# Backward pass of a gated long-convolution block: tile transposes on TensorE, or as DMA transposes

## The chip, the cores and the metric

One Trainium2 chip, one of its cores. The time is the device time of one execution of the whole program, in microseconds (us), as the median of several executions.

A core has these engines: PE (TensorE, matrix multiply, with its own weight loads PEld), DVE (VectorE), ACT (ScalarE), POOL (GpSimd) and SP (SyncE, which here only issues transfers). Sixteen DMA engines per core move data between the chip's main memory (DRAM tensors) and the on-chip SBUF. "PEclk" is the share of TensorE's full clock that the throttle granted. "DMA share" is the mean busy share of the sixteen DMA engines.

## The reference, cut to what matters

The reference computes a block and all its gradients: `jax.vjp` of

```python
xn = layernorm(q)                            # 2048 x 1024
kv = shift_conv(k, shift_k) * v              # 4 taps
y  = irfft(rfft(kv) * rfft(ssm_k)) + kv * ssm_D      # long convolution over 2048
s  = xn * y
g  = silu(((xn @ w_gate) * (xn @ w_up)) @ w_down)    # 1024 -> 3584 -> 1024
out = q + s * g
```

with ten outputs: `out` and nine gradients. Everything is bf16. The Fourier transforms are done as matmuls with cosine and sine tables, so nearly all the arithmetic is TensorE work. In this kernel each matmul takes both operands with the summed axis on the 128 partitions, hence many operands are needed in both orientations; that is where transposes come from.

## The kernel before

Transfers go alternately to two queues, that of SP (hardware issue) and that of POOL (software issue). Each queue is in order.

```python
dma_engs = [nc.sync, nc.gpsimd]
def dma(out, in_, eng=None):        # cut: picks dma_engs in turn
    return eng.dma_start(out=out, in_=in_)
```

All transposes go through one helper: TensorE transposes up to eight 128x128 blocks into PSUM, and ScalarE or VectorE copies each block to SBUF.

```python
def transpose_blocks(pspool, srcs, dst_fn, nblk, tagname):
    for g0 in range(0, nblk, 8):
        nt = min(8, nblk - g0)
        pst = pspool.tile([P, 8 * P], BF16, name=tagname)
        for i in range(nt):
            nc.tensor.transpose(pst[:, i * P:(i + 1) * P], srcs[g0 + i], ident[:])
        for i in range(nt):
            nc.any.tensor_copy(dst_fn(g0 + i), pst[:, i * P:(i + 1) * P])
```

The stages in order of time: layer norm, shift convolution and tables; KV transform (with XNT, the transposed normalised input, built after it); gate and up matmuls; inverse transform; down matmul (`ps_bm`); DY transform (with DBMT, the transposed gradient, built after it); seven groups of the feed-forward backward pass; an inverse transform; the gradient of `w_down` (HH, the transposed hidden tensor) together with the `dk` work; the gradient of the input (`ps_dxn`) in two halves; a last inverse transform.

The first half of a group is called the dh phase here, the second half the dw phase:

```python
for fg in range(FG):                                     # 7 groups
    WDT = fgb.tile([P, DC, 512], BF16, name="WDT")       # one buffer
    for fi in range(4):
        wrow = fgl.tile([P, D], BF16, name="wrow")
        dma(wrow[:], B_w_down[...])
        transpose_blocks(ftps, [... wrow ...], ... WDT ..., DC, "pst_fg")
    DG = ...; DU = ...                                   # [P, NB, 512], one buffer each
    for fi in range(4):                                  # dh phase
        dma(gt_t[:], GTd[frs, :]); dma(ut_t[:], UTd[frs, :])
        for sq in range(SQ):
            # 8 matmuls ps_dh <- WDT, DBMT; ScalarE copies ps_dh to dh_b
            nc.vector.tensor_tensor(dgt[:, cs], dh_b[:], ut_t[:, cs], ALU.mult)
            nc.vector.tensor_tensor(dut[:, cs], dh_b[:], gt_t[:, cs], ALU.mult)
        dma(DGTd[frs, :], dgt[:]); dma(DUTd[frs, :], dut[:])
        for (src, dst) in ((dgt, DG), (dut, DU)):
            transpose_blocks(ftps, [... src ...], ... dst ..., NB, "pst_fg")
        p1_tick(fg * 4 + fi)                             # a slice of the spectral products
    for (src, o_w) in ((DG, o_dwg), (DU, o_dwu)):        # dw phase
        # 128 matmuls ps_dw <- src, XNR each; out to o_w
```

Of the kernel before, what the change touches and what calls it, by code (L numbers as in the profile page):

```python
# [12 lines left out]
BF16 = mybir.dt.bfloat16  # L13
# [4 lines left out]
def build_kernel(  # L18
# [6 lines left out]
    nc = tc.nc  # L25
    P = 128
    _, S, D = A_q.shape
    F = B_w_gate.shape[1]
# [3 lines left out]
    NB = S // P  # L32
    DC = D // P
    FC = F // P
    DH = D // 512
    FG = F // 512
    SQ = S // 512
# [26 lines left out]
    def dma(out, in_, eng=None):  # L64
        if eng is None:
            eng = dma_engs[_dma_ctr[0] % len(dma_engs)]
            _dma_ctr[0] += 1
        return eng.dma_start(out=out, in_=in_)  # L68
# [367 lines left out]
# [8 lines that stand above are left out]
# [139 lines left out]
    XNT = xtp.tile([P, DC, S], BF16, name="XNT")  # L583

    def build_xnt():
        with tc.tile_pool(name="xt_ld", bufs=2) as xtl, \
                tc.tile_pool(name="xt_ps", bufs=2, space=bass.MemoryType.PSUM) as xps:
            for sb in range(NB):
                xn_t = xtl.tile([P, D], BF16, name="xn_l2")
                dma(xn_t[:], XNd[sb * P:(sb + 1) * P, :])  # L590
                transpose_blocks(xps, [xn_t[:, dc * P:(dc + 1) * P] for dc in range(DC)],
                                 lambda i, sb=sb: XNT[:, i, sb * P:(sb + 1) * P], DC, "pst_x")

    with tc.tile_pool(name="kvpool", bufs=1) as kvpool, \
            tc.tile_pool(name="twpool_f", bufs=2) as twpool, \
# [221 lines left out]
    def build_dbmt():  # L817
        for sb in range(NB):
            dma(XNR[:, sb, :], XNd[sb * P:(sb + 1) * P, :])
        with tc.tile_pool(name="db_sb", bufs=3) as dbs, \  # L820
                tc.tile_pool(name="db_ps", bufs=2, space=bass.MemoryType.PSUM) as dps:
            for sb in range(NB):
                rs = slice(sb * P, (sb + 1) * P)
                dbm = dbs.tile([P, D], BF16, name="dbm_l")
                dma(dbm[:], DBMd[rs, :])
                transpose_blocks(dps, [dbm[:, dc * P:(dc + 1) * P] for dc in range(DC)],
                                 lambda i, sb=sb: DBMT[:, i, sb * P:(sb + 1) * P], DC, "pst_db")

    with tc.tile_pool(name="dypool", bufs=1) as dypool, \
            tc.tile_pool(name="twpool_b", bufs=2) as twpool, \  # L830
# [57 lines left out]
    if True:  # L888
        with tc.tile_pool(name="fg_big", bufs=1) as fgb, \
# [7 lines left out]
            for fg in range(FG):  # L897
                f0 = fg * 512
                WDT = fgb.tile([P, DC, 512], BF16, name="WDT")
                for fi in range(4):  # L900
                    wrow = fgl.tile([P, D], BF16, name="wrow")
                    dma(wrow[:], B_w_down[f0 + fi * P:f0 + (fi + 1) * P, :])
                    transpose_blocks(ftps, [wrow[:, ddc * P:(ddc + 1) * P] for ddc in range(DC)],
                                     lambda i, fi=fi, WDT=WDT: WDT[:, i, fi * P:(fi + 1) * P], DC, "pst_fg")
                DG = fgb.tile([P, NB, 512], BF16, name="DG")
                DU = fgb.tile([P, NB, 512], BF16, name="DU")
                for fi in range(4):
# [18 lines left out]
                    dma(DGTd[frs, :], dgt[:])  # L926
                    dma(DUTd[frs, :], dut[:])
                    for (src, dst) in ((dgt, DG), (dut, DU)):
                        transpose_blocks(ftps, [src[:, sb * P:(sb + 1) * P] for sb in range(NB)],
                                         lambda i, dst=dst, fi=fi: dst[:, i, fi * P:(fi + 1) * P], NB, "pst_fg")  # L930
                    p1_tick(fg * 4 + fi)
                for (src, o_w) in ((DG, o_dwg), (DU, o_dwu)):
                    for dc in range(DC):
# [93 lines left out]
    wbcp = tc.alloc_tile_pool(name="wbc_pool", bufs=1)  # L1027
    WBC["t"] = build_wbc(wbcp, "Wbc2")
    with tc.tile_pool(name="dwd_big", bufs=1) as dwb, \
            tc.tile_pool(name="dwd_ld", bufs=2) as dwl, \  # L1030
            tc.tile_pool(name="dwd_out", bufs=2) as dwo, \
            tc.tile_pool(name="dk_sb", bufs=2) as dkp, \
# [8 lines left out]
        for fg in range(FG):  # L1041
            for _ in range(per_fg):
                if dk_blocks:
                    dk_block(dk_blocks.pop(0), dkp, psSH)
            HH = dwb.tile([P, NB, 512], BF16, name="HH")
            for fi in range(4):
                fc = fg * 4 + fi
                ht_t = dwl.tile([P, S], BF16, name="ht_t2")
                dma(ht_t[:], HTd[fc * P:(fc + 1) * P, :])
                transpose_blocks(wtps, [ht_t[:, sb * P:(sb + 1) * P] for sb in range(NB)],  # L1050
                                 lambda i, HH=HH, fi=fi: HH[:, i, fi * P:(fi + 1) * P], NB, "pst_hh")
            for fi2 in range(0, 4, 2):
                pss = [wps.tile([P, D], F32, name=f"ps_dwd{k}") for k in range(2)]
                for sb in range(NB):
# [16 lines left out]
    with tc.tile_pool(name="wt_pool", bufs=1) as wtp, \  # L1071
# [11 lines left out]
        for dh in range(DH):  # L1083
# [1 line left out]
            WGT = wtp.tile([P, FC, 512], BF16, name="WGT")  # L1085
            WUT = wtp.tile([P, FC, 512], BF16, name="WUT")
            for (wsrc, wdst) in ((B_w_gate, WGT), (B_w_up, WUT)):
                for di in range(4):
                    dc = dh * 4 + di
                    wnat = wtl.tile([P, F], BF16, name="wnat")  # L1090
                    dma(wnat[:], wsrc[dc * P:(dc + 1) * P, :])
                    transpose_blocks(wtps, [wnat[:, fc * P:(fc + 1) * P] for fc in range(FC)],
                                     lambda i, wdst=wdst, di=di: wdst[:, i, di * P:(di + 1) * P], FC, "pst_wt")
            for sb in range(NB):
                rs = slice(sb * P, (sb + 1) * P)
                dgt_l = dgl.tile([P, FC, P], BF16, name="dgt_l")
# [137 lines left out]
```

## Time and profile before

3121.07 us, median of 2 runs (3117.57 to 3124.57).

| | before |
|---|---|
| TensorE busy | 88% of the span, granted clock 0.935 |
| ScalarE busy | 1060 us |
| feed-forward groups | 1281.3 to 2018.1 us, 737 us |
| a steady group | 95.7 us, for 384 matmuls of 0.216 us = 82.9 us |

Two parts of the page of the kernel before: busy time by engine, and its DMA queues (packets, MB, share of the sixteen engines' time). q1 is the hardware-issued queue of SP, q0 the software-issued queue of POOL:

```profile
PE 2728.1 (88%) x13818; PEld 1281.9 (41%) x13818; DVE 1626.6 (52%) x3829; ACT 1060.1 (34%) x2938; POOL 626.8 (20%) x1049
q1 hardware_dynamic: 304406, 312.36, 30.9%
q0 software_dynamic: 88400, 312.02, 27.9%
```

The load is even between the two queues, about 312 MB each. The columns of the windows view are: busy time and count by engine, granted clock, DMA share, GB/s.

```profile
core 0: us, PE busy (x) PEld busy (x) DVE busy (x) ACT busy (x) POOL busy (x), PEclk, DMA share, GB/s
1731.80:1768.90 37.10, 36.02 (x244) 18.52 (x244) 21.93 (x77) 27.18 (x95) 4.82 (x9) 1.00 0.63 203
1769.80:1826.60 56.80, 56.62 (x278) 26.25 (x278) 2.80 (x12) 14.03 (x36) 4.86 (x9) 1.00 0.20 72
```

The reader is to see that the group's mean share of 0.36 is made of 0.63 and 0.20.

### The profile page before, as it was taken

The numbers are of one execution on the slowest core, as the hardware profiler recorded it, in microseconds if no ns is written. First come the engines' busy times: TensorE is split into PE (matmuls) and PEld (weight loads), VectorE is DVE, ScalarE is ACT, GpSimd is POOL, SyncE is SP. The second block draws the span as 40 slices with busy tenths as digits, with TensorE's granted clock in tenths as the row PEclk, the third lists the DMA queues.
The fourth block names the chain that finished last, engine by engine and source line by source line (L and its number), as shares of the span: only waits on it lengthen the run. The fifth ranks groups of instructions, "written<-read, shape, count | busy, mean of one in ns | idle before, by whom it ended". The sixth has DMA issues, their size and how long they took to land. (4 is left out here: it accounts for less than half of the span.)

```text
span 3117.5 us, 39882 instructions
## 1 busy us (share of the span) xinstructions
PE 2728.1 (88%) x13818; PEld 1281.9 (41%) x13818; DVE 1626.6 (52%) x3829; ACT 1060.1 (34%) x2938; POOL 626.8 (20%) x1049
## 2 busy tenths in 40 slices
PE   4949899999799979799899999878899599889888
PEld 2413344444344434444444444433444344444333
DVE  7977778111255751299953331184997460034461
ACT  6512433333101113545535543300555530242222
POOL 2221132222334320112110110133221111112200
PEclk8978999999899989899999999998999689889988
DMA  7795595343748882588644432266875685558602
GB/s 250 286 334 193 193 322 216 145 167 117 280 156 288 284 295 102 185 299 280 214 168 140 141 127 92 94 224 208 296 264 178 213 250 158 161 162 244 210 25 84
DMA packets 393008, 626.92 MB, mean 201 GB/s; under 512 B 147795, under 2 KB 260435, under 8 KB 388964
## 3 DMA queue, kind: packets, MB, share of 16 engines
q1 hardware_dynamic: 304406, 312.36, 30.9%
q0 software_dynamic: 88400, 312.02, 27.9%
q8 instruction: 108, 1.77, 0.2%
q14 instruction: 94, 0.77, 0.1%
HBM read 406.89 MB, written 221.55 MB: 202 GB/s over the span
## 5 line engine op out<-in xcount | busy, mean ns | idle before, releaser
L429 PE MATMUL psI<-YSh,TWR 128*128 128x512 bf16 x1536 | 355.9, 391 | 69.5 <-DVE TWR L217 19.1
L688 PE MATMUL psG<-XNT,wg_s 128*128 128x512 bf16 x896 | 342.7, 383 | 11.3 <-ACT g_b L691 6.8
L689 PE MATMUL psU<-XNT,wu_s 128*128 128x512 bf16 x896 | 342.6, 382 | 3.2 <-DMA wu_s<-in_B_w_up_dram 3.0
L1105 PE MATMUL ps_dxn<-WGT,dgt_l 128*128 128x512 bf16 x896 | 341.6, 382 | 0.0
L1105 PE MATMUL ps_dxn<-WUT,dut_l 128*128 128x512 bf16 x896 | 340.9, 381 | 0.2 <-DMA dut_l<-DUTd 0.2
L936 PEld LDWEIGHTS <-XNR 128*128 128x128 bf16 x1792 | 174.9, 98 | 212.7 <-issue 9.1
L429 PEld LDWEIGHTS <-TWR 128*128 128x128 bf16 x1536 | 152.2, 100 | 262.0 <-issue 64.5
L920 PE MATMUL ps_dh<-DBMT,WDT 128*128 128x512 bf16 x896 | 221.3, 390 | 9.8 <-ACT WDT L443 8.7
L1058 PE MATMUL ps_dwd<-DBM,HH 128*128 128x512 bf16 x896 | 206.2, 382 | 12.1 <-ACT HH L443 7.4
L936 PE MATMUL ps_dw<-DG,XNR 128*128 128x512 bf16 x896 | 199.9, 381 | 3.9 <-ACT w_b L939 3.0
L756 PE MATMUL ps_bm<-WD,ht_t 128*128 128x512 bf16 x896 | 195.7, 381 | 3.7 <-DMA ht_t<-HTd 3.7
L936 PE MATMUL ps_dw<-DU,XNR 128*128 128x512 bf16 x896 | 194.9, 379 | 1.6 <-ACT w_b L939 1.5
L695 DVE TENSOR_TENSOR h_b<-g_b,u_b 128x512 bf16<-128x512 bf16 x112 | 47.4, 423 | 225.6 <-ACT u_b L693 225.6
L939 ACT CAST w_b<-ps_dw 128x512 bf16<-128x512 f32 x112 | 65.3, 584 | 267.3 <-PE ps_dw L936 257.7
L691 ACT CAST g_b<-psG 128x512 bf16<-128x512 f32 x112 | 65.5, 585 | 256.4 <-PE psG L688 239.7
L689 PEld LDWEIGHTS <-wu_s 128*128 128x128 bf16 x896 | 88.3, 99 | 117.7 <-issue 10.8
L688 PEld LDWEIGHTS <-wg_s 128*128 128x128 bf16 x896 | 88.2, 98 | 112.3 <-issue 8.7
L443 ACT COPY HH<-pst_hh 128x128 bf16<-128x128 bf16 x441 | 117.2, 266 | 50.0 <-PE pst_hh L441 38.0
L756 PEld LDWEIGHTS <-ht_t 128*128 128x128 bf16 x896 | 87.7, 98 | 111.7 <-issue 4.6
L1105 PEld LDWEIGHTS <-dut_l 128*128 128x128 bf16 x896 | 88.0, 98 | 106.6 <-issue 1.6
L1105 PEld LDWEIGHTS <-dgt_l 128*128 128x128 bf16 x896 | 88.1, 98 | 105.2 <-issue 1.1
L1058 PEld LDWEIGHTS <-HH 128*128 128x128 bf16 x896 | 84.7, 98 | 110.8 <-ACT HH L443 15.2
(341 smaller groups left out, 4574.9 us busy)
## 6 DMA issues: line engine op xcount, KB each, us to landing
kt<-KPAD SPq DMA_DIRECT2D x64, 256.0 KB, 5.2
kt<-KPAD POOLq DMA_DIRECT2D x64, 256.0 KB, 5.0
dgt_l<-DGTd SPq DMA_DIRECT2D x16, 896.0 KB, 11.5
dut_l<-DUTd POOLq DMA_DIRECT2D x16, 896.0 KB, 8.8
dgt_l<-DGTd POOLq DMA_DIRECT2D x16, 896.0 KB, 8.4
dut_l<-DUTd SPq DMA_DIRECT2D x16, 896.0 KB, 8.1
KVFd<-kvf_t POOLq DMA_DIRECT2D x6, 1536.0 KB, 6.0
pp_kvf<-KVFd SPq DMA_DIRECT2D x12, 768.0 KB, 9.7
```

What stands on the lines that cost most here:

```text
L429: nc.tensor.matmul(ps[:], tws2[c][:, gb * P:(gb + 1) * P], YSh[:, gb, par, c, :], start=(i_mm == 0), stop=(i_mm == nmm - 1))
L443: nc.any.tensor_copy(dst_fn(g0 + i), pst[:, i * P:(i + 1) * P])
L688: nc.tensor.matmul(psG[:], wg_s[:, dc, fi * P:(fi + 1) * P], rhs, start=(dc == 0), stop=(dc == DC - 1))
L689: nc.tensor.matmul(psU[:], wu_s[:, dc, fi * P:(fi + 1) * P], rhs, start=(dc == 0), stop=(dc == DC - 1))
L691: nc.scalar.copy(out=g_b[:], in_=psG[:])
L695: nc.vector.tensor_tensor(h_b[:], g_b[:], u_b[:], ALU.mult)
L756: nc.tensor.matmul(ps[:, dh * 512:(dh + 1) * 512], lhsT, WD[:, fc, dh * 512:(dh + 1) * 512], start=(fc == 0), stop=(fc == FC - 1))
L920: nc.tensor.matmul(ps[:], WDT[:, ddc, fi * P:(fi + 1) * P], DBMT[:, ddc, cs], start=(ddc == 0), stop=(ddc == DC - 1))
L936: nc.tensor.matmul(ps[:], XNR[:, sb, dc * P:(dc + 1) * P], src[:, sb, :], start=(sb == 0), stop=(sb == NB - 1))
L939: nc.scalar.copy(out=w_b[:], in_=ps[:])
L1058: nc.tensor.matmul(pss[k][:, dh * 512:(dh + 1) * 512], HH[:, sb, fi * P:(fi + 1) * P], DBM[:, sb, dh * 512:(dh + 1) * 512], start=(sb == 0 ...
L1105: nc.tensor.matmul(ps[:], lt[:, fc, :], wt[:, fc, :], start=(i_acc == 0), stop=(i_acc == n_acc - 1))
```

## The change

The intent: let the DMA crossbar do the transposes while data moves, so that TensorE, PSUM and the copies on ScalarE and VectorE are freed of them. 2272 TensorE transposes and as many copies become 82 transposing DMAs, all issued by SP. The core of the diff (index arithmetic cut):

```diff
 def build_xnt():
-    for sb in range(NB): dma(xn_t[:], XNd[...]); transpose_blocks(... XNT ..., "pst_x")
+    for sg in range(SQ):
+        nc.sync.dma_start_transpose(out=XNT[:, :, sg*512:(sg+1)*512], in_=XNd[sg*512:(sg+1)*512, :])
 def build_dbmt():
-    for sb in range(NB): dma(dbm[:], DBMd[rs, :]); transpose_blocks(... DBMT ..., "pst_db")
+    for sg in range(SQ):
+        nc.sync.dma_start_transpose(out=DBMT[:, :, sg*512:(sg+1)*512], in_=DBMd[sg*512:(sg+1)*512, :])
 # in each group
-    for fi in range(4): dma(wrow[:], ...); transpose_blocks(... WDT ..., "pst_fg")
+    nc.sync.dma_start_transpose(out=WDT[:], in_=B_w_down[f0:f0 + 512, :])
     ...
-            transpose_blocks(ftps, [... src ...], ... dst ..., NB, "pst_fg")
+            nc.sync.dma_start_transpose(out=dst[:, :, fi*P:(fi+1)*P], in_=src[:])
 # w_down gradient
-    HH = dwb.tile(...)                       # one buffer
-    for fi in range(4): dma(ht_t[:], HTd[...]); transpose_blocks(... HH ..., "pst_hh")
+    HH = dwb2.tile(...)                      # two buffers
+    nc.sync.dma_start_transpose(out=HH[:], in_=HTd[fg * 512:(fg + 1) * 512, :])
 # input gradient
     for (wsrc, wdst) in ((B_w_gate, WGT), (B_w_up, WUT)):
-        for di in range(4): dma(wnat[:], ...); transpose_blocks(... wdst ..., "pst_wt")
+        nc.sync.dma_start_transpose(out=wdst[:], in_=wsrc[dsl, :])
```

More of the change, by code (lines that the diff above doesn't have):

```diff
@@ L585, in build_xnt @@
     def build_xnt():
-        with tc.tile_pool(name="xt_ld", bufs=2) as xtl, \
-                tc.tile_pool(name="xt_ps", bufs=2, space=bass.MemoryType.PSUM) as xps:
-            for sb in range(NB):
-                xn_t = xtl.tile([P, D], BF16, name="xn_l2")
-                dma(xn_t[:], XNd[sb * P:(sb + 1) * P, :])
-                transpose_blocks(xps, [xn_t[:, dc * P:(dc + 1) * P] for dc in range(DC)],
-                                 lambda i, sb=sb: XNT[:, i, sb * P:(sb + 1) * P], DC, "pst_x")
+        for sg in range(SQ):
+            nc.sync.dma_start_transpose(out=XNT[:, :, sg * 512:(sg + 1) * 512],
+                                        in_=XNd[sg * 512:(sg + 1) * 512, :])
     with tc.tile_pool(name="kvpool", bufs=1) as kvpool, \
@@ L819, in build_dbmt @@
             dma(XNR[:, sb, :], XNd[sb * P:(sb + 1) * P, :])
-        with tc.tile_pool(name="db_sb", bufs=3) as dbs, \
-                tc.tile_pool(name="db_ps", bufs=2, space=bass.MemoryType.PSUM) as dps:
-            for sb in range(NB):
-                rs = slice(sb * P, (sb + 1) * P)
-                dbm = dbs.tile([P, D], BF16, name="dbm_l")
-                dma(dbm[:], DBMd[rs, :])
-                transpose_blocks(dps, [dbm[:, dc * P:(dc + 1) * P] for dc in range(DC)],
-                                 lambda i, sb=sb: DBMT[:, i, sb * P:(sb + 1) * P], DC, "pst_db")
+        for sg in range(SQ):
+            nc.sync.dma_start_transpose(out=DBMT[:, :, sg * 512:(sg + 1) * 512],
+                                        in_=DBMd[sg * 512:(sg + 1) * 512, :])
     with tc.tile_pool(name="dypool", bufs=1) as dypool, \
@@ L899, in build_kernel @@
                 WDT = fgb.tile([P, DC, 512], BF16, name="WDT")
-                for fi in range(4):
-                    wrow = fgl.tile([P, D], BF16, name="wrow")
-                    dma(wrow[:], B_w_down[f0 + fi * P:f0 + (fi + 1) * P, :])
-                    transpose_blocks(ftps, [wrow[:, ddc * P:(ddc + 1) * P] for ddc in range(DC)],
-                                     lambda i, fi=fi, WDT=WDT: WDT[:, i, fi * P:(fi + 1) * P], DC, "pst_fg")
+                nc.sync.dma_start_transpose(out=WDT[:], in_=B_w_down[f0:f0 + 512, :])
                 DG = fgb.tile([P, NB, 512], BF16, name="DG")
@@ L928, in build_kernel @@
                     for (src, dst) in ((dgt, DG), (dut, DU)):
-                        transpose_blocks(ftps, [src[:, sb * P:(sb + 1) * P] for sb in range(NB)],
-                                         lambda i, dst=dst, fi=fi: dst[:, i, fi * P:(fi + 1) * P], NB, "pst_fg")
+                        nc.sync.dma_start_transpose(out=dst[:, :, fi * P:(fi + 1) * P], in_=src[:])
                     p1_tick(fg * 4 + fi)
@@ L1029, in build_kernel @@
     with tc.tile_pool(name="dwd_big", bufs=1) as dwb, \
+            tc.tile_pool(name="dwd_big2", bufs=2) as dwb2, \
             tc.tile_pool(name="dwd_ld", bufs=2) as dwl, \
@@ L1044, in build_kernel @@
                     dk_block(dk_blocks.pop(0), dkp, psSH)
-            HH = dwb.tile([P, NB, 512], BF16, name="HH")
-            for fi in range(4):
-                fc = fg * 4 + fi
-                ht_t = dwl.tile([P, S], BF16, name="ht_t2")
-                dma(ht_t[:], HTd[fc * P:(fc + 1) * P, :])
-                transpose_blocks(wtps, [ht_t[:, sb * P:(sb + 1) * P] for sb in range(NB)],
-                                 lambda i, HH=HH, fi=fi: HH[:, i, fi * P:(fi + 1) * P], NB, "pst_hh")
+            HH = dwb2.tile([P, NB, 512], BF16, name="HH")
+            nc.sync.dma_start_transpose(out=HH[:], in_=HTd[fg * 512:(fg + 1) * 512, :])
             for fi2 in range(0, 4, 2):
@@ L1087, in build_kernel @@
             for (wsrc, wdst) in ((B_w_gate, WGT), (B_w_up, WUT)):
-                for di in range(4):
-                    dc = dh * 4 + di
-                    wnat = wtl.tile([P, F], BF16, name="wnat")
-                    dma(wnat[:], wsrc[dc * P:(dc + 1) * P, :])
-                    transpose_blocks(wtps, [wnat[:, fc * P:(fc + 1) * P] for fc in range(FC)],
-                                     lambda i, wdst=wdst, di=di: wdst[:, i, di * P:(di + 1) * P], FC, "pst_wt")
+                nc.sync.dma_start_transpose(out=wdst[:], in_=wsrc[dsl, :])
             for sb in range(NB):
```

## The prediction

> **What bounds the kernel now.** I read four views in this order: the page, the busy time of each engine by stage, the timeline of TensorE, the waits. The page says TensorE is busy 88% of the span, but its matmuls overlap, so I take no gap from that figure. The windows view cuts the span at the stage borders that the tile names give:
>
> ```profile
> core 0: us, PE busy (x) PEld busy (x) DVE busy (x) ACT busy (x) POOL busy (x), PEclk, DMA share, GB/s
> ...
> 1195.00:1281.00 86.00, 86.00 (x400) 39.02 (x399) 0.00 (x0) 26.61 (x50) 4.32 (x8) 1.00 0.27 104
> 1281.00:1414.00 133.00, 110.95 (x674) 57.25 (x672) 108.98 (x349) 67.81 (x258) 27.75 (x44) 0.92 0.82 281
> ...
> 1731.00:1827.00 96.00, 94.56 (x553) 46.40 (x551) 24.93 (x89) 43.03 (x136) 9.68 (x18) 1.00 0.36 121
> 2183.00:2437.00 254.00, 231.40 (x1339) 111.99 (x1338) 209.98 (x243) 139.65 (x466) 50.15 (x94) 0.99 0.66 228
> 2437.00:2513.00 76.00, 36.36 (x255) 26.09 (x254) 48.80 (x161) 49.64 (x186) 12.06 (x15) 0.57 0.84 283
> 2513.00:2705.00 192.00, 191.82 (x899) 87.14 (x898) 37.45 (x114) 16.28 (x26) 27.03 (x21) 1.00 0.64 178
> 2705.00:2754.00 49.00, 28.12 (x226) 22.87 (x224) 14.81 (x66) 37.38 (x148) 3.06 (x4) 0.55 0.46 151
> ```
>
> The reader is to see two kinds of stretch. Where TensorE has operands (1195 to 1281, 2513 to 2705) it is full at a clock of 1.00. Where it transposes weights (2437 to 2513, 2705 to 2754) it is half idle and the granted clock is 0.57 and 0.55. The timeline gives the rate: in the DY transform 423 matmuls of 512 columns take 91.46 us, 216 ns each; that is my unit for useful work.
>
> Transposes cost TensorE little by themselves when they lie between matmuls. A steady feed-forward group of the backward pass runs 1731.8 to 1827.5, 95.7 us, with 128 + 256 matmuls = 384 x 0.216 = 82.9 us. So 160 transposes (32 for WDT, 128 for DG and DU) and their waits cost 12.8 us, 80 ns each. Their copies are on ScalarE and VectorE:
>
> ```profile
> L443 ACT COPY HH<-pst_hh 128x128 bf16<-128x128 bf16 x441 | 117.2, 266 | 50.0 <-PE pst_hh L441 38.0
> ...
> L441 PE MATMUL pst_wt<-ident,wnat 128*128 128x128 bf16 x448 | 51.8, 300 | 55.7 <-ACT WGT L443 14.0 <-DVE WUT L443 10.9 <-ACT WUT L443 8.0
> ...
> L443 ACT COPY WUT<-pst_wt 128x128 bf16<-128x128 bf16 x169 | 39.0, 274 | 11.2 <-PE pst_wt L441 8.3
> ```
>
> At some 270 ns a copy on ScalarE and 224 ns on VectorE, 224 copies (one half of WGT and WUT) take 224 / (1/0.27 + 1/0.224) = 27 us with both engines on them, and 49 us as they ran. There the copies, not the transposes, hold TensorE.
>
> **What the Trainium skill says.** "VectorE: DVE Perf Modes", section The three transpose paths, gives 390 ns for a 128x128 bf16 transpose on TensorE and 1309 ns on the crossbar, for one alone. The trace has sixteen in a row in 1.06 us, 66 ns each, so the isolated figure does not apply in a stream; for the crossbar I likewise want a rate. "DMA: Bandwidth & Descriptors", section Latency and other measured facts, has 261 GB/s measured for DMA transposes with a non-contiguous middle dimension, 350 to 400 when contiguous. No transpose DMA is in this trace; the destinations here are three-dimensional, so I take 261. The same page, section DMA Transpose (X-bar), allows only hardware-generated issue; hence all of them go through the Sync queue, one stream, beside half of all other transfers. "TensorE: Matmul & The Clock Gate", section Why this matters for your kernels, warns of gaps above some 3 us between matmuls. The trace agrees: after an idle 3.1 us at 1416.7 the next five matmuls took 2.31 us, 462 ns each instead of 216.
>
> **The change part by part.** Removed: 128 (XNT) + 128 (DBMT) + 224 (WDT) + 896 (DG, DU) + 448 (HH) + 448 (WGT, WUT) = 2272 transposes and as many copies, about 570 us of ScalarE and VectorE time at 0.25 us. Added: 82 transposing DMAs. For all but DG and DU they replace a load of the same bytes (45 MB); DG and DU add 56 x 512 KB = 29 MB, an estimated 113 us of the DMA engines at 261 GB/s against 737 us of that stage, whose DMA share is 0.36 when steady. So bandwidth is there; what counts is what waits.
>
> XNT. XNd is written by about 160 us, the transposes (4.2 MB, 16 us) can run under the KV transform: hidden. From the timeline, TensorE did 288 matmuls (62 us) between 296.6 and 384.5, 26 us lost to pst_x, its copies and slow restarts; from 384.5 to 420.4 it did 16 us of gate/up matmuls, 20 lost, of which 10 remain because the first wu_s lands only at 394.7. I count 30 of these 36 as gained.
>
> DBMT and group 0. DBMd is complete at 1195 and the DY transform leaves the DMA engines at 0.27: hidden. From 1281.3 to 1414.3 are 133 us for 82.9 of matmuls.
>
> The groups. WDT (1 MB, 4 us) can be fetched under the 55 us of dw matmuls. DG and DU for the first three row blocks of a group are hidden too, but dw needs the last one, and this wait is new. Last dh matmul, copy of dh_b and dgt product: 1.1 us (1864.7 to 1865.8). A store of 128 KB lands in 1.7 us, of which 0.4 is transfer at 330 GB/s: 1.3 fixed. The transpose of 512 KB: 2.0 us at 261 GB/s, up to 3 more as it shares the engines with the 1 MB of DGTd and DUTd stores issued at the same time. Then matmuls restart at half rate for about 4 us, 2 lost. Together about 10 us per group, E. DU comes behind the 28 us of DG matmuls, hidden. So a steady group goes from 12.8 to 10 lost: four groups gain 11. Groups 1 and 2 (105.8 and 115.2 us) lose 23 and 32, because their copies queue behind the spectral products on VectorE (101 of the 106 us from 1414 to 1520 busy); dgt and dut still do, 5 us each: gains 8 and 17. Group 0 loses 50, afterwards 10 + 10: gain 30.
>
> HH. A group takes 36.0 us (2209.8 to 2245.9) for 128 matmuls, 27.7 us. With HH by DMA (2 MB, 8 us, two buffers) TensorE needs 896 x 0.216 = 194 us and would end near 2378. But VectorE runs the dk work without a gap from 2187.6 to 2396.1, so that becomes the end of the stage. Its finish took 11 us (2437.4 to 2448.7), so the loads of WGT and WUT, which take over that memory, begin at about 2407 instead of 2450: 43 us earlier.
>
> WGT, WUT, first half. 7.3 MB at 261 GB/s is 28 us. The engines are already at 0.98 in 2440 to 2482 with the products' and dgt/dut loads, so I take 45, plus 2 for the restart: full matmul rate from 2454. Now it comes at 2513, with 2.4 us of matmuls done before: gain 57, the shift of 43 included. Second half: one buffer each, so the transposes begin when the last matmul of the first half ends, and nothing hides them: 28 + 1.5 + 5 of sharing + 2 = 36.5 against 47.3 now (2704.7 to 2754.2 less 2.2 of matmuls): gain 11.
>
> Sum: 30 + 30 + 8 + 17 + 11 + 57 + 11 = 164 us; 3121 - 164 = 2957, I say 2960.
>
> **The rivals.** First, a DMA wait in place of a copy wait: E. For it: every group has one point where dw waits for bytes made 1 us before, and before it waited only for copies that flowed block by block. If E is 6, the seven groups give 28 us more; if it is 15, 35 less, and the steady groups become slower than now. Second, the crossbar or its single queue as the bound: at half my rate the two unhidden weight fills cost 28 us more each and E 2 to 4 more per group, about 80 in all: 3040. The queue could also hold back dgt_l loads behind the fills. Against: the four hidden places need 4 to 16 us within 28 to 90. Third, VectorE keeps the time: if the dk chain and the spectral products set these stages, only WGT, WUT, XNT and DBMT gain. For it: 210 of 254 us busy in the HH stage; against: its copies fall away too, and the chain ends 41 us before TensorE does. Fourth, all is hidden and restarts are short: 2900.
>
> **Range and chances.** Good ends of E (28) and of the weight fills without sharing (17 + 5) give about 2905; the slow crossbar gives 3040; with slack for rescheduling, 2885 to 3055. Faster by over 2% means below 3059: only a crossbar well under half of 261 GB/s misses that. Faster 0.86, within 2% 0.11, slower 0.03.
>
> **What would show it.** TensorE going from the DY transform to ps_dh without a gap; dh-to-dw gaps of 6 to 9 us with DG waiting for a DMA, followed by matmuls over 400 ns; steady groups of 92 to 94 us; dk ending near 2396 less the earlier gains and bounding its stage; the fills of WGT and WUT landing 28 to 45 us after issue, and 34 to 40 us of idle TensorE between the halves. It would be wrong if transposes of 512 KB land later than 8 us, if 3.7 MB takes over 30 us, if ordinary loads on the Sync queue starve behind them, or if the new order of instructions moves the spectral products onto the path.

## The result, and the profile after

3209.44 us, median of 2 runs (3208.06 to 3210.83), against 3121.07: the changed kernel is slower, ratio 1.0294 with a 95% interval of 1.0241 to 1.0346. A ratio here is the one that the comparison of the runs gave, with its interval; it is not quite the ratio of the medians quoted (1.0283). The mean granted clock fell from 0.935 to 0.903. The outputs stayed correct.

The same two parts of the page, of the changed kernel:

```profile
PE 2567.1 (80%) x11318; PEld 1138.2 (35%) x11546; DVE 1525.2 (48%) x3341; ACT 646.2 (20%) x1154; POOL 596.4 (19%) x997
q1 hardware_dynamic: 590358, 364.27, 40.8%
q0 software_dynamic: 82832, 289.47, 26.1%
```

The removal worked as meant: ScalarE lost 414 us of work, VectorE 101 us, TensorE 161 us. The span grew by 92 us all the same. The SP queue's packets nearly doubled.

From the timeline of TensorE, the borders of the stages and what each took:

| stretch | before | after | gain | predicted |
|---|---|---|---|---|
| start to KV transform | 232.2 | 251.0 | −19 | 0 |
| KV transform to end of gate/up | 568.0 | 568.9 | −1 | +30 |
| to end of DY transform | 481.1 | 496.7 | −16 | 0 |
| group 0 | 133.0 | 159.9 | −27 | +30 |
| groups 1 and 2 | 221.0 | 240.3 | −19 | +25 |
| groups 3 to 6 | 382.8 | 421.8 | −39 | +11 |
| inverse transform | 164.7 | 165.1 | 0 | 0 |
| HH stage and first fill of WGT, WUT | 330.2 | 301.9 | +28 | +57 |
| input gradient, second fill included | 432.6 | 432.3 | 0 | +11 |
| rest | 171.9 | 171.1 | +1 | 0 |
| sum | 3117.5 | 3209.1 | −92 | +164 |

A steady group, cut at its own border into dh phase and dw phase, as is the steady group of the kernel before in the windows view above. The header line is the one shown above:

```profile
1932.80:1983.40 50.60, 29.25 (x126) 12.56 (x128) 11.72 (x32) 9.85 (x17) 4.79 (x9) 0.83 0.95 255
1983.40:2038.80 55.40, 55.14 (x252) 25.14 (x258) 0.00 (x0) 8.78 (x15) 4.34 (x8) 1.00 0.16 52
```

The dw phase is as long as before. The dh phase grew from 37.1 to 50.6 us while its TensorE work shrank, and its DMA share rose from 0.63 to 0.95. The timeline of TensorE over this phase (start, duration, what, count, and in brackets the idle time before it and what ended it):

```profile
1932.76 21.10 PE L907 MATMUL ps_dh<-DBMT,WDT 128*128 128x512 bf16 x95
1957.54 5.34 PE L907 MATMUL ps_dh<-DBMT,WDT 128*128 128x512 bf16 x23 [3.67 <-ACT dh_b L910]
1980.14 3.00 PE L907 MATMUL ps_dh<-DBMT,WDT 128*128 128x512 bf16 x7 [17.26 <-DMA WDT<-in_B_w_down_dram]
1983.40 6.86 PE L922 MATMUL ps_dw<-DG,XNR 128*128 128x512 bf16 x31 [0.26 <-DMA DG<-dgt]
```

The seven matmuls after the wait of 17.26 us belong to the next group: the scheduler put them ahead of the dw matmuls, so they wait for the next WDT. DG arrives almost at the same moment (0.26 us later), so either of the two would have held TensorE. What the SP queue did in the same stretch:

```profile
1958.88 0.57 SPq L68 DMA_DIRECT2D gt_t<-GTd  x1
1959.55 6.70 SPq L916 DMA_TRANSPOSE DG<-dgt  x1
1966.34 0.53 SPq L68 DMA_DIRECT2D DUTd<-dut  x1
1966.92 3.00 SPq L916 DMA_TRANSPOSE DU<-dut  x1
1969.97 1.61 SPq L68 DMA_DIRECT2D ut_t<-UTd  x1
1971.68 6.27 SPq L891 DMA_TRANSPOSE WDT<-in_B_w_down_dram  x1
1978.05 0.53 SPq L68 DMA_DIRECT2D DGTd<-dgt  x1
1978.63 2.79 SPq L916 DMA_TRANSPOSE DG<-dgt  x1
1981.51 1.67 SPq L916 DMA_TRANSPOSE DU<-dut  x1
```

A plain transfer mostly holds the queue for some 0.5 us and then runs on its own. A transpose of 512 KB holds it for 1.67 to 6.70 us here. VectorE, which makes dgt and dut, had to wait for its own loads in this phase, and finished the last dgt of the group at 1967.0:

```profile
1956.03 0.42 DVE L911 TENSOR_TENSOR dgt<-dh_b,ut_t 128x512 bf16<-128x512 bf16 x1 [9.34 <-DMA ut_t<-UTd]
...
1964.87 0.43 DVE L912 TENSOR_TENSOR dut<-dh_b,gt_t 128x512 bf16<-128x512 bf16 x1 [5.24 <-DMA gt_t<-GTd]
```

The last DG, whose data were then ready, was issued only at 1978.63, behind DU, a load, WDT and a store. While TensorE waited for WDT, from its issue to its landing, the DMA engines moved 348 GB/s, more than the 255 of the phase as a whole:

```profile
1971.70:1980.10 8.40, 0.00 (x0) 0.00 (x0) 0.00 (x0) 0.00 (x0) 0.00 (x0) 0.50 1.13 348
```

The DMA share is 1.13 here: as the profile counts it, it is not capped at 1, so a share near 1 says that the engines are busy, but not by itself that nothing more would fit. The tile view of the late groups (duration of the hold in ns, minimum, median and maximum; then the time from issue to landing, which the trace gives for only seven of these 20) says how long one takes:

```profile
L916 SPq DMA_TRANSPOSE DG<-dgt x20: 2297/5290/8646, 1615.7 to 2074.9; - x20
...
DMA to landing us min/median/max: 4.6/9.4/10.4
```

The groups of all dh matmuls and of the dw matmuls on DG, from the page (busy, mean ns, idle time before and what ended it):

```profile
L907 PE MATMUL ps_dh<-DBMT,WDT 128*128 128x512 bf16 x879 | 217.1, 408 | 157.8 <-DMA WDT<-in_B_w_down_dram 111.7
L922 PE MATMUL ps_dw<-DG,XNR 128*128 128x512 bf16 x877 | 203.2, 392 | 48.2 <-DMA DG<-dgt 44.4
```

In the kernel before these two rows have 9.8 and 3.9 us of idle time, so the idle time before them rose by 192 us. The groups became only 85 us longer, mainly because their 1120 TensorE transposes, an estimated 90 us at the 80 ns each that the prediction found, are gone. Of the 85 us, 46 were lost in groups 0 to 2, where the spectral products run as well; the steady group shown here stands for the other 39.

### The profile page after: what moved, and what is told of

Read it like the earlier page. It is cut to its first block, busy times and chain, and to the rows that moved or that the text cites. A ratio compares the mean times of both kernels' runs of the same rounds, so it can differ in the third digit from the quotient of the medians. Undisturbed runs are those within 1.5% of the kernel's fastest.

```text
span 3209.1 us, 32738 instructions
## 1 busy us (share of the span) xinstructions
PE 2567.1 (80%) x11318; PEld 1138.2 (35%) x11546; DVE 1525.2 (48%) x3341; ACT 646.2 (20%) x1154; POOL 596.4 (19%) x997
## 4 chain that ended last, share of the span: by engine, by line
PE 24%; issue 11%; DMA 7%; DVE 5%; SPq 4%; POOL 1%; ACT 0%; POOLq 0%; DVEq 0%; ACTq 0%
PE ps_dxn L1082 10%; PE ps_dw L922 6%; PE psI L429 5%; SPq L1070 2%; PE ps_dwd L1040 1%; PE ps_dh L907 1%; DMA gt_t<-GTd 1%; DMA dksh<-DKSHd 1%; DVE prodf L993 1%; SPq L916 1%; DMA DG<-dgt 1%; DMA ut_t<-UTd 1%; DMA dgt_l<-DGTd 1%; DMA WUT<-in_B_w_up_dram 0%; POOL out_dram L68 0%
## 5 line engine op out<-in xcount | busy, mean ns | idle before, releaser
L1082 PE MATMUL ps_dxn<-WUT,dut_l 128*128 128x512 bf16 x861 | 329.1, 382 | 13.9 <-DMA WUT<-in_B_w_up_dram 12.0
L684 PE MATMUL psG<-XNT,wg_s 128*128 128x512 bf16 x860 | 329.2, 383 | 13.1 <-ACT g_b L687 7.9
L911 DVE TENSOR_TENSOR dgt<-dh_b,ut_t 128x512 bf16<-128x512 bf16 x112 | 47.2, 422 | 407.8 <-ACT dh_b L910 343.1
L1040 PE MATMUL ps_dwd<-DBM,HH 128*128 128x512 bf16 x878 | 204.4, 391 | 44.8 <-ACT wd_b L1045 36.4
L907 PEld LDWEIGHTS <-WDT 128*128 128x128 bf16 x896 | 91.8, 103 | 280.4 <-issue 94.9
L925 ACT CAST w_b<-ps_dw 128x512 bf16<-128x512 f32 x112 | 65.2, 584 | 432.6 <-PE ps_dw L922 420.8
```

The source lines that it names most:

```text
L684: nc.tensor.matmul(psG[:], wg_s[:, dc, fi * P:(fi + 1) * P], rhs, start=(dc == 0), stop=(dc == DC - 1))
L907: nc.tensor.matmul(ps[:], WDT[:, ddc, fi * P:(fi + 1) * P], DBMT[:, ddc, cs], start=(ddc == 0), stop=(ddc == DC - 1))
L925: nc.scalar.copy(out=w_b[:], in_=ps[:])
L1040: nc.tensor.matmul(pss[k][:, dh * 512:(dh + 1) * 512], HH[:, sb, fi * P:(fi + 1) * P], DBM[:, sb, dh * 512:(dh + 1) * 512], start=(sb == 0 ...
L1082: nc.tensor.matmul(ps[:], lt[:, fc, :], wt[:, fc, :], start=(i_acc == 0), stop=(i_acc == n_acc - 1))
```

## The experiments

Twelve kernels ran, all correct. The texts quoted as expected use these names. A: the transposes hold the in-order SP queue, so that other loads come late; order is the cause. B: the crossbar or the DMA engines are too slow. C: the single WDT buffer and the scheduler's order. E: in the dh phase the DMA engines are full, and what is moved there at that moment must wait (the prediction uses the same letter for something else, the wait per group). P: the prediction's own account. Each ratio is to the kernel before on the same chip; that kernel's medians were 3118.73, 3117.57, 3117.27 and 3117.21 us.

### One part of the change alone (three runs)

The parts of the diff were applied singly: XNT and DBMT; WDT, DG and DU; HH, WGT and WUT.

```diff
 # e1: only these two of the change's hunks; the rest as before
+        nc.sync.dma_start_transpose(out=XNT[...], in_=XNd[...])
+        nc.sync.dma_start_transpose(out=DBMT[...], in_=DBMd[...])
```

> The kernel before with only XNT and DBMT transposed by DMA. Theory A (a transpose DMA holds the Sync queue until it is nearly done, so the loads behind it come late, and no matmul was waiting for the transposes it removes in the KV transform): the KV transform starts some 19 us late, as in the changed kernel, the DY transform another 15 to 19 us late, and only group 0 of the feed-forward backward gets 15 to 30 us back; total 3125 to 3145 us. Rival P (the prediction: both are hidden and give 60 us together): 3060 us. Rival B (the changed kernel loses only in the feed-forward groups and at the weight fills): 3060 to 3100 us, with no delay of the KV and DY transforms.

Measured: 3130.97 us, ratio 1.0046 (1.0018 to 1.0073). The KV transform began at 253.5 us and the DY transform ran from 1186.3 to 1315.3, so both delays of the changed kernel are there, from these two hunks alone.

```diff
 # e2: only these hunks
+                nc.sync.dma_start_transpose(out=WDT[:], in_=B_w_down[f0:f0 + 512, :])
+                        nc.sync.dma_start_transpose(out=dst[:, :, fi*P:(fi+1)*P], in_=src[:])
```

> The kernel before with only WDT, DG and DU transposed by DMA. Theory A: this carries most of the loss, since one in-order queue has to carry 9 transposes of 5.2 MB per group in some 45 us beside half of the loads; the stage goes from 737 us to 810 to 840, the total to 3190 to 3225 us. Rival P: 3060 to 3100 us. If the loss comes from the interplay with DBMT on the same queue instead, 3121 to 3160 us.

Measured: 3248.06 us, ratio 1.0412 (1.0381 to 1.0443), a miss: slower than the range expected and slower than the whole change. The groups took from 1282.6 to 2156.9, 874 us, against 822 in the changed kernel. The dh phase of group 0 alone took 118 us (1296.0 to 1414.1), against 79 in the changed kernel and 59 before.

```diff
 # e3: only these hunks
+            HH = dwb2.tile([P, NB, 512], BF16, name="HH")
+            nc.sync.dma_start_transpose(out=HH[:], in_=HTd[fg * 512:(fg + 1) * 512, :])
+                nc.sync.dma_start_transpose(out=wdst[:], in_=wsrc[dsl, :])
```

> The kernel before with only HH, WGT and WUT transposed by DMA. Theory A: as in the changed kernel, the HH stage gains about 12 us and the two weight fills about 16, total 3085 to 3100 us. Rival P (HH stage bound by VectorE alone, fill of 45 us from there): 3121 minus 68, 3053 us. If parts do not add up to the 88 us of the whole change, this one differs by more than 20 us from 3093.

Measured: 3096.89 us, ratio 0.9931 (0.991 to 0.9952), as expected: this part gains 22 us.

What follows from the three: the loss is in the groups, and the first and last stages account for little of it. The parts do not add up: 12 + 129 − 22 = 119 us against some 90 for all of them. DBMT by DMA makes group 0 cheaper when WDT, DG and DU go by DMA as well; why was not tested.

### Plain transfers off the SP queue (two runs)

If holding the queue were the whole cause, a queue that carries nothing but transposes should cure it. All plain transfers that alternate went to POOL, in the changed kernel and, as a control, in the kernel before.

```diff
-    dma_engs = [nc.sync, nc.gpsimd]
+    dma_engs = [nc.gpsimd]
```

> The changed kernel with every plain load and store that alternated between Sync and GpSimd now issued by GpSimd, so the Sync queue carries next to nothing but the transposes. To be read against the kernel before with the same edit (the next run). Theory A (loads queued behind transposes in the Sync queue): KV and DY transforms start as in that control, TensorE no longer waits some 4 us for ut_t and gt_t per group, and the wait for WDT falls from 17 us to under 10; changed minus control lies between -40 and +20 us instead of +88. Rival B (the crossbar or the DMA engines are too slow, whoever issues the loads): the difference stays +60 to +90 us.

> Control: the kernel before with all alternating loads and stores issued by GpSimd. No theory needs a change here; GpSimd's 0.54 us an issue may cost something: 3115 to 3180 us.

Measured: the changed kernel 3416.8 us, ratio 1.0956 (1.0896 to 1.1015); the control 3131.66 us, ratio 1.0044 (1.0025 to 1.0064). The control shows that one queue for plain transfers costs only 14 us by itself. With the transposes beside it the same edit cost the changed kernel 207 us (3416.8 less 3209.44, in two calls). The expectation of A was wrong, in its parts too: the KV transform began at 298.7 us and the DY transform at 1250.1, where the control has 230.1 and 1154.3 and the changed kernel 251.0 and 1194.4, and single waits for WDT reached 28.1 us. VectorE's waits for ut_t did fall, from 45.7 us in the groups to 18.5. By the same borders as in the table above, the profiled execution is 224 us longer than that of the changed kernel: 48 before the KV transform, 29 up to the end of the DY transform, 35 in the groups, 71 in the HH stage with the first fill, 63 in the input gradient; the other stages gave back 22. So most of this loss is not in the groups. The page of this run and the windows view of one of its groups:

```profile
q0 software_dynamic: 165664, 578.94, 51.3%
q1 hardware_dynamic: 293766, 74.80, 18.2%
...
2020.00:2079.00 59.00, 29.80 (x127) 12.78 (x129) 11.81 (x32) 9.97 (x17) 9.03 (x17) 0.76 0.96 229
```

The dh phase is again at a DMA share of 0.96. Here q1 holds only transposes (and a few tiny loads), so their rate can be read: 74.80 MB in 18.2% of 3432.7 us is 120 GB/s of engine time, while the plain transfers of q0 get 578.94 MB in 51.3%, 329 GB/s. Its packets are 255 bytes on average (74.80 MB over 293766), those of q0 3.5 KB. A transpose of WDT held its queue for 6.27 us in the group shown above and for 14.03 us in this phase, with nothing but transposes in its queue; but these are single cases. Over all groups the median hold of WDT went from 7.66 to 9.81 us and that of DU from 2.71 to 4.45, while that of DG fell from 5.97 to 3.63. What the run shows is that plain transfers standing behind transposes in one queue are not the whole cause, since the loss stays without them. That the transposes are slow because of what runs beside them is argued, not shown: WDT is held 4.40 us in the median of the best kernel below, where DG and DU are not moved by DMA, but the few known landings of WDT do not differ much (8.4, 9.9 and 15.7 us in the changed kernel, 9.1 and 9.4 in the run with WDT alone). Whether small packets wait for their turn among large ones was not isolated.

### WDT alone, DG and DU alone (two runs)

```diff
 # e6: only
+                nc.sync.dma_start_transpose(out=WDT[:], in_=B_w_down[f0:f0 + 512, :])
 # e7: only
+                        nc.sync.dma_start_transpose(out=dst[:, :, fi*P:(fi+1)*P], in_=src[:])
```

> The kernel before with only WDT transposed by DMA, DG and DU by TensorE. Theory A (WDT is late because DG's and DU's transposes hold the queue before it): WDT is fetched under the dw matmuls or shortly after the last dh matmul, 0 to 8 us of wait per group, total 3100 to 3140 us. Rival C (WDT's single buffer is the cause: it can only start when the last dh matmul is done, and the schedule puts the next group's dh before dw): TensorE waits 10 us or more for WDT in each group also here, 3160 us or more.

> The kernel before with only DG and DU transposed by DMA, WDT by TensorE. Theory A: the queue is held some 30 us per group, gt_t and ut_t come late and the last DG is waited for: 10 to 18 us lost per group, little gained: 3160 to 3220 us. Rival C: with WDT out of the queue there is only the predicted wait of some 8 us for the last DG, which the removed transposes pay for: 3090 to 3130 us.

Measured: WDT alone 3111.2 us, ratio 0.9979 (0.9948 to 1.001); DG and DU alone 3206.36 us, ratio 1.0305 (1.0271 to 1.0338). A steady group of WDT alone, dh and dw phase:

```profile
1800.00:1835.00 35.00, 34.46 (x181) 16.39 (x183) 7.15 (x24) 12.15 (x33) 3.25 (x6) 1.00 0.23 75
1835.00:1892.00 57.00, 55.92 (x320) 27.73 (x326) 15.32 (x55) 25.68 (x81) 5.92 (x11) 1.00 0.49 158
```

TensorE is full in both and the clock is 1.00: the WDT transposes are hidden, so the single buffer and the transposing load are not enough for a wait. The other half of C, the scheduler's order, is not tested by this run: here no dh matmuls of the next group stand ahead of dw, as they do in the changed kernel and in the run with WDT, DG and DU. It is the second run that speaks against C. There WDT comes from TensorE, no TensorE wait for a WDT transfer is left (only 33.3 us in all groups for its copies, 8.7 before), and yet DG and DU alone cost 89 us, where C expected 3090 to 3130. Their dh phases are 39 to 53 us in the four late groups, against 38 before, and before the dw matmuls there are gaps of up to 12.3 us for DG; groups 0 to 2 lost more still (dh phases of 88, 61 and 63 us against 59, 45 and 47). These 56 transposes of 512 KB cost as much by themselves as the whole change.

### Stores out of the dh phase (two runs)

E says that the dh phase must move too much at once: loads of gt and ut, stores of dgt and dut, and the transposes of both. The stores are not urgent. They were kept back until the last DU transpose of the group had been issued. This needed four buffers for dgt and dut; to make room, one pass shared a tile, and in the second run wrow had one buffer as well. The stores, which had alternated between the two queues, all go to SP here.

```diff
-                    dgt = fgl.tile(...); dut = fgl.tile(...)
+                    dgt = fgs.tile(...); dut = fgs.tile(...)       # own pool, 4 buffers
-                    dma(DGTd[frs, :], dgt[:]); dma(DUTd[frs, :], dut[:])
+                    late += [(DGTd[frs, :], dgt), (DUTd[frs, :], dut)]
 ...
+                with tc.issue_after(last_t.ins):                   # the group's last DU transpose
+                    for (dst_d, src_t) in late:
+                        nc.sync.dma_start(out=dst_d, in_=src_t[:])
```

On the changed kernel:

> The changed kernel with the stores of DGTd and DUTd (4.2 MB a group) issued only behind the group's last transpose, so under the dw matmuls, where the DMA engines stand at 0.16. Theory E (in the dh phase the DMA engines are full, 0.94 to 0.95[...]): the phase loses half of its plain bytes and goes from 51 us to about 36 to 40 in the steady groups, total 3209 - 70 to - 110, 3100 to 3140 us. Theory A (only the order in the Sync queue, loads behind transposes, counts): the loads stay where they are in that queue, the phase gains under 5 us a group, 3175 us or more.

Measured: 3172.7 us, ratio 1.017 (1.0145 to 1.0195); 37 us less than the changed kernel's median, between the two expectations and far nearer to A's (3175 or more) than to E's (3100 to 3140), so it does not decide for E. A steady group:

```profile
1807.50:1851.00 43.50, 28.79 (x129) 12.46 (x127) 11.81 (x32) 9.96 (x17) 2.69 (x5) 0.87 0.92 200
1851.10:1907.40 56.30, 56.30 (x257) 25.37 (x258) 0.00 (x0) 8.79 (x15) 3.81 (x7) 0.98 0.35 126
```

The dh phase fell from 50.6 to 43.5 us, and the stores now fill the empty dw phase (0.35 instead of 0.16). What remains is one wait of 14.58 us for the next WDT, which stands in the same full phase.

On the kernel with DG and DU alone, where no WDT transposes stand in the way:

> The kernel of e7 (only DG and DU by DMA, WDT by TensorE, 1.0305 of before) with the stores of DGTd and DUTd behind the group's last transpose. Theory E (DMA engines full in the dh phase): with WDT and the stores out of it the phase falls from 48 to 59 us to 36 to 40, about that of before, ratio 1.000 to 1.010. Theory A (loads behind transposes in the one queue; that order is unchanged): 1.020 or more.

Measured: 3146.48 us, ratio 1.0094 (1.0069 to 1.0119), as E expected, from 1.0305 without the edit. The late groups' dh phases take 32 to 41 us; the start of the dw matmuls in one of them, and the windows line of its dh phase:

```profile
1804.05 8.14 PE L939 MATMUL ps_dw<-DG,XNR 128*128 128x512 bf16 x31 [5.07 <-DMA DG<-dgt]
...
1764.20:1804.00 39.80, 30.13 (x156) 13.56 (x153) 11.87 (x34) 16.77 (x45) 3.77 (x7) 0.99 1.00 214
```

With stores and WDT transposes out of the way the wait for DG is 5.07 us here and up to 7.2 in the other late groups. The DMA share of the phase is still 1.00, so the engines stayed busy; what changed is what they, and the SP queue, were busy with when the last DG came. The 29 us still lost lie mainly in groups 0 and 1, whose dh phases take 86 and 58 us against 59 and 45 before. The edit takes bytes out of the phase and commands out of the queue at once, and it gives dgt and dut four buffers instead of two: in the groups of the changed kernel VectorE waited 18.9 us for DG transposes to free a dgt. It does not say how much each of the three is worth; the buffers alone were not tried.

### The early transposes issued behind the loads (one run)

In the two early stages the transposes have time but stand in the SP queue ahead of loads that are needed sooner. They were issued after those loads, which still alternate between the two queues.

```diff
+                kv_i = dma(KVs[...], par_rows(KVd, sigma, ub), ...)
     def build_xnt():
+      with tc.issue_after(kv_i.ins):
         ... nc.sync.dma_start_transpose(out=XNT[...] ...)
+                dy_i = dma(DYs[...], par_rows(DYd, sigma, ub), ...)
     def build_dbmt():
+        with tc.issue_after(dy_i.ins):
             ... nc.sync.dma_start_transpose(out=DBMT[...] ...)
```

> The kernel of the first experiment (only XNT and DBMT by DMA, 1.0046 of before) with these transposes queued on Sync behind the loads of KV and of DY. Theory A (there the loads came late because they stood behind transposes): the KV transform starts at 232 us again and the DY transform within 5 us of before, and group 0 keeps its gain: ratio 0.990 to 0.996 of before, 3090 to 3105 us. Theory E alone (the engines full, not the order): little changes, 1.000 to 1.005.

Measured: 3106.23 us, ratio 0.9962 (0.9947 to 0.9978), against 1.0046 for the same two parts in their first order. The KV transform starts at 232.3, as before the change. The first DY matmul, in the changed kernel and then in this one, shows the other half:

```profile
1194.40 5.36 PE L256 MATMUL psN<-DY,altcol 128*1 128x512 bf16 x16 [22.38 <-DMA DY<-DYd]
```

```profile
1159.61 2.29 PE L256 MATMUL psN<-DY,altcol 128*1 128x512 bf16 x5 [4.68 <-DMA DY<-DYd]
```

And this is what the wait of 22.38 us was, in the SP queue of the changed kernel:

```profile
1164.08 12.50 SPq L817 DMA_TRANSPOSE DBMT<-DBMd  x1
...
1177.37 13.92 SPq L817 DMA_TRANSPOSE DBMT<-DBMd  x1
1191.65 0.33 SPq L68 DMA_DIRECT2D DY<-DYd  x1
```

Two transposes of 1 MB held the queue for 26 us, and the loads of DY came behind them: the eight of these loads that POOL issues began at 1172.3, the eight of SP at 1191.65. For DY A is right: the late loads are the ones behind the transposes.

For KV the same edit gave the 19 us back, but A is not shown there. In the changed kernel the KV loads went out late on both queues, at 245.7 on SP and here on POOL:

```profile
L68 POOL DMA_DIRECT2D KV<-KVd x8: 536/536/536, 245.2 to 254.1; - x8
```

Before the change they began at 227.1 and 226.6. The last XNT transpose had left the queue at 179.0, and with no plain transfers behind the transposes (the run above with all of them on POOL) the KV transform began later still. In the stretch from 60 to 180 us the DMA share was 0.91 against 0.79 before, so the 4.2 MB moved there are a rival cause; this edit removes both, the bytes and the place in the queue.

### The weight fills fetched early, and a version of all that gains (two runs)

The first halves of WGT and WUT need 7.3 MB of memory and nothing that the kernel computes. They got a pool of their own and were issued in the inverse transform ahead of the HH stage. The second halves went by DMA too, at their old place (cut below); HH stayed on TensorE.

```diff
+    wtp = tc.alloc_tile_pool(name="wt_pool", bufs=1, side="right")
+    WT0 = [wtp.tile([P, FC, 512], BF16, name=n) for n in ("WGT", "WUT")]
 ...  # after the loads of DBM, in the inverse transform
+        for (wsrc, wdst) in ((B_w_gate, WT0[0]), (B_w_up, WT0[1])):
+            nc.sync.dma_start_transpose(out=wdst[:], in_=wsrc[0:512, :])
```

> The kernel before with WGT and WUT transposed by DMA only, the first halves into memory of their own and issued before the HH stage, HH by TensorE. If transposes by DMA are worth what they are where the engines have room and the result is not waited for, the first fill of 68 us vanishes but for some 10, the second goes from 47 to about 38: 3121 - 65 = 3055 us (3035 to 3075). If they slow the transfers of the HH stage as much as they hide, 3090 us or more.

Measured: 3072.47 us, ratio 0.9846 (0.9829 to 0.9862), inside the expected range. The input gradient starts at 2457.8 us; in the kernel before it reached its full rate at 2513.

Then a combination of what had gained: these early fills, the second fill cut in four chunks so that matmuls can start on the first, WDT by DMA, and DBMT by DMA behind the loads of DY. XNT, DG, DU and HH stayed on TensorE.

```diff
 # e11 = early fills + WDT + DBMT after the DY loads, and for the second half:
+            for k in range(0 if dh == 0 else 4):
+                for (wsrc, wdst) in ((B_w_gate, WGT), (B_w_up, WUT)):
+                    nc.sync.dma_start_transpose(out=wdst[:, 7*k:7*k+7, :],
+                                                in_=wsrc[dsl, 896*k:896*k+896])
```

> The transposes by DMA only where the engines have room and nothing waits at once: WGT and WUT (first halves before the HH stage as in e9, second halves in four chunks each so that matmuls can start on the first), WDT alone in the feed-forward stage, DBMT queued behind the loads of DY. Sum of the parts: e9 -45, DBMT of e10 -13, WDT of e6 -10, chunks -15: 3121 - 83 = 3035 us, ratio 0.970 to 0.978. If the parts get in each other's way, 0.980 to 0.985.

Measured: 3033.75 us (3030.38 to 3046.61), ratio 0.9744 (0.972 to 0.9768), inside the expected range. It beats the kernel before by 2.6% and the changed kernel by about 5.5% (3033.75 over 3209.44). Its steady groups take 92.9 us (1814.6 to 1907.5), and both phases have a clock of 1.00.

## Why the prediction was wrong

**The step that failed** is "an estimated 113 us of the DMA engines at 261 GB/s against 737 us of that stage, whose DMA share is 0.36 when steady. So bandwidth is there; what counts is what waits." The mean over a group hides that two thirds of its engine time lie in the dh phase. That phase had a share of 0.63 over 37.1 us, 23.4 us of all engines' time. Adding the 4.2 MB of DG and DU of one group at the prediction's own 261 GB/s makes 16.1 us more, 39.5 us in all, for a phase of 37.1. By its own numbers the phase was full before any wait was counted. The runs show 0.95, 0.96, 0.92 and 1.00 in this phase in the four kernels with DG and DU by DMA whose windows are shown. In the steady group the phase took 50.6 us instead of 37.1, 17.26 of them in a wait for WDT with the engines at 348 GB/s. That DG and DU in this phase are the cause is shown by the run with them alone (+89 us) and by the late stores, which took that to +29. How much of it is bytes, how much order in the queue and how much buffers was not measured.

**E, the new wait**, was sized 10 us per group: "The transpose of 512 KB: 2.0 us at 261 GB/s, up to 3 more as it shares the engines". A steady group now loses 105.9 − 82.9 = 23 us, of which 3.67 + 17.26 + 0.26 are the three waits shown and the rest slow restarts (the seven matmuls after the long wait took 3.00 us, some 1.5 lost, where the prediction took 2). The prediction's terms make 3.3 to 6.3 us from issue to landing; the median of the seven known DG landings is 9.4, over the 8 that the prediction itself had named as a sign of being wrong. And the issue itself came 11.6 us after the data were ready (1967.0 to 1978.63), because others of its kind stood ahead of it; the sum had no term for that. With the stores and WDT out of the phase the size of about 10 fits: the run with DG and DU alone and late stores has 5 to 7 us before the restart. Rival 1 had the direction ("if it is 15, 35 less, and the steady groups become slower than now"), but not 23.

**Hidden, twice**: "XNd is written by about 160 us, the transposes (4.2 MB, 16 us) can run under the KV transform: hidden", and likewise DBMT. No matmul waited for these transposes, but KV and DY came late: −19 and −16 us, and the reordered run gave both back. For DY the cause is the in-order queue, for KV it stays open between the queue and the 4.2 MB more in a stage whose DMA share was already 0.79. The danger of the queue stands in the prediction's last sentence ("if ordinary loads on the Sync queue starve behind them"), but it has no term in the sum.

**XNT's gain of 30** did not come either: the KV transform takes 152.3 us before and 152.4 after, and gate/up 410.4 and 411.3. Taking the transposes and copies of XNT out from between its matmuls freed nothing, so the 26 us counted there were not theirs. The trace of the changed kernel shows what stands there now: TensorE waits three times, 18.3 us in all, for ScalarE's copies kvf_t out of PSUM (once, 3.9 us, before), and ScalarE in turn waits 34.5 us in that stretch for VectorE's products ypi_m. VectorE is busy 62.7 of 84.4 us there and 63.5 of 84.5 before, so its chain is the likely limit in both; no run took it away.

**Groups 0 to 2** lost 46 where 55 were to be gained. The copies are gone from behind the spectral products, as foreseen, but the same busy phase takes their place. In group 0, where TensorE was to go over from the DY transform without a gap, it waits 20.81 us for WDT, 19.62 for dh_b and 27.25 for DG; the DMA share of its dh phase is 1.06. The split for groups 1 and 2 was not settled.

**The HH stage**: 28 gained of 57. "VectorE runs the dk work without a gap … so that becomes the end of the stage", 43 us earlier. The first fill was issued at 2552.76, 249 us after the first HH matmul, instead of about 267 before: 18 gained. A transpose of 2 MB held the SP queue for 8 to 17 us and landed after 18.0 and 20.8 in the two cases that the trace gives, where 8 was estimated. Before they ran, HH transposes also stood 51.9 us at the head of the SP queue until TensorE had freed a buffer, and nothing behind them was issued. TensorE waited 36.4 us for ScalarE's copies wd_b, and these 40.7 us for earlier stores of wd_b; VectorE lost 25.7 us on loads of dksh. The SP queue at the fill that follows:

```profile
2552.76 16.82 SPq L1070 DMA_TRANSPOSE WGT<-in_B_w_gate_dram  x1
...
2570.25 29.15 SPq L1070 DMA_TRANSPOSE WUT<-in_B_w_up_dram  x1
2599.81 0.38 SPq L68 DMA_DIRECT2D dgt_l<-DGTd  x1
```

The matmuls began at 2605.66, 52.9 us after the issue of WGT, where 45 + 2 were predicted: near. But the last thing waited for was dgt_l, an ordinary load behind the two fills, which rival 2 had named ("hold back dgt_l loads behind the fills").

**Right**: WDT is hidden, shown by the run with it alone. The second fill leaves TensorE 38 us without work (25.96 + 12.02), where 36.5 was predicted; but slow restarts and a late load cost some 7 us in the two halves (432.3 less 387.1 of matmuls and 38), so the stage gained nothing. The work removed from ScalarE and VectorE is gone as counted: 515 us less busy on the two, 570 predicted. Rival 2, the slow crossbar and its single queue, came nearest to the mechanism, and was priced at 3040 because it was applied only to the waits already in the sum.

**What stays open**: how much of a DG transpose's slowness in the dh phase is the engines' share-out between small and large packets and how much is the queue; what the buffers of dgt and dut are worth; why KV came late; why the parts do not add up; why the run with all plain transfers on POOL lost most outside the groups.

## What to carry to other kernels

Before moving work to the DMA engines, cut the profile at the phase in which the transfer must run, and add the new bytes to the share of that phase, not to the mean of the stage. A DMA transpose belongs where the engines are idle and nothing urgent stands behind it in its queue: weights fetched one stage early, with the second halves by DMA as well, gained 45 us here. Transposes between matmuls cost TensorE some 80 ns each with their waits, and for data that is made a microsecond before its use that was cheaper here than the transfers tried.

## What the Trainium skill lacked or had wrong

- "DMA: Bandwidth & Descriptors", section DMA Transpose (X-bar), gives no time for which a transpose on this chip holds its in-order queue, many microseconds in which nothing behind it is issued. The SP queue shows 0.3 to 0.6 us for most plain transfers, and for transposes 1.67 to 17.5 us (512 KB), 3.9 to 13.9 us (1 MB), 8.1 to 17.2 us (2 MB) and 13.3 to 29.2 us (3.67 MB). The prediction had no term for it.
- The same page, section Latency and other measured facts, has 261 GB/s for transposes with a non-contiguous middle dimension, and no figure for transposes beside other traffic. Here they got 120 GB/s of engine time over a whole run in which plain transfers got 329, and a DG of 512 KB took 9.4 us from issue to landing in the median of the seven landings known (4.6 at best).
- "Advanced Engine Details and Errata", section X-Bar Transpose (TRN2), says that "TRN2 transpose DMAs are as fast as regular DMAs". In the company of regular ones they were not: the two rates just given differ by a factor of 2.7. No run here measured one alone.
